# Splitting the last gather of a recurrent step into two column halves in two PSUM banks, with new issue orders, in a memory-augmented attention kernel (forward and backward)

## The chip, the cores and the metric

The kernel runs on 1 core of one Trainium2 chip. The metric is the device time of one execution in microseconds (us); lower is better. The engines named below are TensorE (PE for its matmuls, PEld for its weight loads), VectorE (DVE), ScalarE (ACT), GpSimd (POOL) and SyncE (SP); SP and POOL also issue DMA transfers, each from its own in-order queue.

## The reference, cut to what matters

The program computes a layer and the gradients of its inputs and weights: `x + A(norm(x)) + B(norm(x))`, where B is a dense layer with squared ReLU and A is attention over 64 segments of 32 tokens that hand eight memory rows from segment to segment.

```python
for s in range(n_seg):                       # 2048 / 32 = 64 segments
    h = jnp.concatenate([mem, xs], axis=1)   # 8 memory rows + 32 tokens, 512 columns
    q, k, v = h @ Wq, h @ Wk, h @ Wv         # 32 heads of 128
    p = _softmax(where(mask, q @ k.T * scale, -1e9))
    o = einsum('bhte,hed->btd', p @ v, Wo)
    mem = o[:, :M, :].copy()                 # M = 8: the next segment needs this
    outs.append(o[:, M:, :])
```

The memory rows make A a chain: a segment cannot begin its projections before the one ahead of it has finished its output projection. The gradient runs the same chain from the last segment to the first: the gradient of the eight memory rows of segment s is an input of segment s-1.

## The kernel before, in words

The program has five stages. The first normalises x and does layer B; a short one projects rows that no chain needs first. Then comes the forward chain (64 steps, one per segment), a middle stage with the rest of the attention gradient's preparation and B's weight gradients, the backward chain (64 steps), and at the end the weight gradients of A as 128 long products.

A step keeps 32 rows of one segment for four groups of eight heads, stacked to 128 partitions. Most matmuls are therefore packed: four matmuls with 32 output partitions each stand side by side in the array (`tile_position=(0, 32 * g)`), 512 columns wide. Sixteen of them make up one call of `proj` or `gather` for one half of the heads; the text calls that a unit.

A forward step is written as named operations: `k0mm k1mm q0mm q1mm v0mm v1mm` (projections, L392), `..ev` (their copies out of PSUM), `..fl` and `..Te` (turning by TensorE, L165, and copying), `s0 s1` (scores), `mx sb ex su rc pm tu` (softmax and turning of one half), `w0 w1` (products with v, L547), `oa ob` (their copies), `g0 g1` (the output projection, `gather`, L460: both halves accumulate into one PSUM tile `ps_R` of 128 x 512), `ra rb` (the copies of its two column halves to `R4`, L374 and L377, one on DVE, one on ACT), `ta tb` (two float32 turns each, L469, into the tile `ps_sum`), `HT` (the sum over the four groups of heads for the eight memory rows, written straight into the input `X` of the next step, L482) and `xt` (the same for the other rows). A backward step ends the same way: six units of `gather` (`vg kg qg`, two each) accumulate into one tile `ps_gR`, then `ra rb ta tb HT`, and the sum goes to `GT`, the input of the step that follows. Ahead of that stand `o0mm o1mm` (projection of the incoming gradient), `vp kp qp` (products), `d1 d2 d3 d4` (the softmax gradient) and the copies `ve vl ke kl qe`.

Rows that only need a block of four steps are handled by operations with the prefix `L.`: they belong to no step's chain. Their matmuls are fill for TensorE: in a forward block six projections `L.P0` to `L.P5`, two gathers `L.G0 L.G1`, `L.S W ta tb BT`; in a backward block twelve half units `L.G0` to `L.I3` and one pair of turns.

Nothing decides the order of issue at run time. `F_ORDER` and `B_ORDER` are four strings each, one per step of a block, and `play` calls the operations in the order of the strings; every engine executes its own share in that order. A `+` behind a name takes the operation of one step (or block) later, a `-` of one earlier. `ENGS` says whether a copy goes to ACT or DVE. POOL copies `pb` (the probabilities into the block-diagonal tile `PD`, which `vp` needs) and `vc`, and issues the loads `ldp ldq ldn`; SP issues the others, `vtr` and `ldk` among them. Single-buffered tiles make some of these wait: `ldq` for the last `kp` of the step ahead, `vc` for its scores, `pb` for its `vp`.

PSUM has eight banks. Four are the pool `r` (every `big` and `tr` tile: projections, scores, `ps_R`, `ps_sum`), four are the two pairs `pp0` and `pp1` for `w`, `vp`, `kp` and `qp`.

Of the kernel before, what the change touches and what calls it, by code (L numbers as in the profile page):

```python
# [26 lines left out]
def kernel(  # L27
# [372 lines left out]
    def heads_of(W):  # L400

        return lambda h: W[:, h, :]
# [50 lines left out]
    def gather(R, XT, W, h, first, last):  # L453

        for k in range(4 * h, 4 * h + 4):
            for g in range(HG):
                x, o = W(g * KH + k), R[32 * g:32 * g + 32, :]
                if len(x.shape) == 3:
                    o = o.rearrange("p (a b) -> p a b", b=P)
                nc.tensor.matmul(o, lhsT=XT(k, g), rhs=x,  # L460
                                 start=(first and k == 4 * h), stop=(last and k == 4 * h + 3),
                                 tile_position=(0, 32 * g))

# [117 lines left out]
    def play(order, n, steps, lefts, step, blk, done=None):  # L581
# [22 lines left out]
        "tb ta L.E0 HT",  # L604
        "L.W1 L.ob0 L.out- k0mm L.oa0 L.oa1 L.ob1 q0mm soP- L.E1 q1mm k0ev k1mm q0ev k0fl xt- q1ev k1ev k0Te q0fl "
        "q0Te q1fl k1fl k1Te L.hs s0 mx0 sb0 q1Te s1 v0mm mx1 sb1 ex0 v0ev su0 rc0 pm0 L.lq+ L.lp ex1 tu0 v1mm "
        "soN- su1 L.otr rc1 pm1 tu1 w0 v1ev ob0 L.P2 oa0 L.X0 w1 L.lo ob1 g0 oa1 g1 soP rb L.P3 km L.t3 ra tb ta "
        "soN HT",
        "k1mm q0mm k0mm L.E3 L.E2 kl L.sx- xt- q0ev k1ev q1mm k0ev k0fl q0fl q1ev k0Te L.hl++ k1fl q0Te L.u3 k1Te "
        "q1fl s0 mx0 q1Te s1 sb0 mx1 sb1 ex0 L.ldL+ ex1 su0 rc0 pm0 tu0 v0mm su1 v0ev rc1 pm1 v1mm L.X1 w0 v1ev "  # L610
        "tu1 oa0 ld L.G1 w1 soV- ob0 L.t2 km ob1 oa1 L.mtr g0 g1 ra L.P5 soP rb L.E5 tb ta HT",
        "L.G0 k0mm xt- L.ra q0mm kl q1mm k1mm k0ev q0ev k0fl q1ev k1ev q0fl k0Te q1fl q0Te k1fl L.u2 s0 q1Te "
        "L.lv+ L.lb k1Te L.t1 L.ta s1 mx0 sb0 mx1 sb1 v0mm ex0 ex1 v0ev v1mm su0 rc0 pm0 v1ev L.mst L.tb tu0 su1 "
        "w0 rc1 ob0 L.P4 pm1 tu1 L.xt oa0 L.E4 w1 oa1 soV- soN- g0 ob1 g1 km rb soV ra kl+ L.S0+ tb ta L.X2 soP "
        "L.u1 HT xt L.mx0+ L.S1+ L.sb0+ k0mm+ L.mx1+ q0mm+ L.sb1+ k1mm+ q1mm+ q0ev+ k0ev+ k1ev+ ld q1ev+ soN "
        "L.ex0+ k0fl+ q0fl+ k1fl+ k0Te+ q1fl+ q0Te+ L.ex1+ q1Te+ k1Te+ s0+ mx0+ v0mm+ sb0+ L.t0 L.su1+ ex0+ L.lm+ "
        "su0+ km+ s1+ mx1+ sb1+ v0ev+ ex1+ v1mm+ L.P0+ rc0+ v1ev+ pm0+ tu0+ ld++ w0+ oa0+ su1+ rc1+ pm1+ ob0+ "
        "L.P1+ tu1+ w1+ ld+ ob1+ L.su0+ L.rc0+ L.pm0+ oa1+ L.u0 L.rc1+ g0+ L.pm1+ g1+ soV+ L.tu0+ rb+ L.tu1+ "
        "L.W0+ L.BT ra+ kl++")
    ENGS = on_engines(  # L620
        "L.E1 L.E2 L.E4 L.oa0 L.ob0 k0ev k1ev oa0 ob0 ob1 q1Te q1ev rb v0ev v1ev",
        "L.E0 L.E3 L.E5 L.oa1 L.ob1 L.pm0 L.pm1 L.ra k0Te k1Te oa1 pm0 pm1 q0Te q0ev ra")
    with sb("fw", 1) as fw, psum("fr", 4) as fr, psum("fpp", 1) as fpp, \
# [182 lines left out]
        def fwd(s):  # L806
# [50 lines left out]
            for p in range(2):  # L857
# [21 lines left out]
                def G_(p=p):  # L879
                    if "R" not in ps:  # L880
                        ps["R"] = big("ps_R")
                        ps["n"] = 0
                    ps["n"] += 1
                    gather(ps["R"], lambda k, g: B_["OT"][:, g, k, j, :], heads_of(Wo), p, ps["n"] == 1, ps["n"] == 2)
                o["g%d" % p] = G_

            def ra(h):
                if "R4" not in st:
                    st["R4"] = fo.tile([P, D], F32, name="R4", tag="R4s")
                c = slice(h * 2 * P, (h + 1) * 2 * P)  # L890
                ENGS["r%s" % "ab"[h]](st["R4"][:, c], ps["R"][:, c])
            o["ra"], o["rb"] = lambda: ra(0), lambda: ra(1)
            turn_ops(o, big, lambda: st["R4"], st)

            def HTf():
                if s + 1 < NSEG:
                    b1, j1 = divmod(s + 1, SPB)
                    over_groups(block(b1)["X"][:, :, j1 * SEG:j1 * SEG + M], st["T"], slice(0, M))
            o["HT"] = HTf
            o["xt"] = lambda: over_groups(B_["XT"][:, :, j, M:SEG], st["T"], slice(M, SEG))  # L900
# [36 lines left out]
    with sb("la", 2) as la, sb("ls", 2) as ls, sb("lo", 1) as lo_, sb("wg", 2) as wg, psum("lpp", 1) as lpp, psum("lr", 4) as lr:  # L937
# [151 lines left out]
        "L.ko1 kg0 d41 qea0 L.G2 qeb0 tu1 qg0 kla0 qp1 klb0 L.I1 qea1 qeb1 kp1 qg1 keb1 kea1 klb1 kg1 rb ra L.H1 "  # L1089
        "tb kla1 vtr ta ldq HT",  # L1090
        "L.H2 o0mm L.ra1 vc- pb- o0ev o1mm L.ktr o0fl o0te o1ev vp0 ldk- xt- s0 L.kst d10 d20 vea vp1 d30 vla "
        "o1fl d40 vtr vlb vg0 veb kp0 vc tu0 vtr+ o1te ldp qp0 qeb0 s1 qea0 d11 d21 kea0 keb0 d31 vg1 qg0 kla0 "
        "klb0 d41 kg0 kp1 tu1 kea1 qp1 L.I3 keb1 qeb1 kg1 qea1 qg1 rb ra L.I2 L.vtr tb ta HT",
        "L.G3 o0mm ldn- ldk- L.ra2 o0ev kla1- o1mm o1ev ldp o0fl pb- xt- klb1- vp0 o0te s0 vea L.gs d10 vp1 vla "
# [11 lines left out]
    with sb("bq", 1) as bq, sb("bt", 1) as bt, sb("bs", 2) as bs, sb("be", 1) as be, psum("bpp", 1) as bpp, psum("br", 4) as br:  # L1106
# [111 lines left out]
        def bwd(s):  # L1218
# [40 lines left out]
            for p in range(2):  # L1259
# [51 lines left out]
                for t, n in ((2, "v"), (1, "k"), (0, "q")):  # L1311
# [13 lines left out]
                    def G_(n=n, p=p, t=t):  # L1325
                        if "R" not in ps:
                            ps["R"] = big("ps_gR")
                            ps["n"] = 0
# [215 lines left out]
```

## Time and profile before

| | |
|---|---|
| runs | 3069.1 us median of 3 (3064.48 to 3072.56) |
| span of the profiled execution | 3059.8 us (no other time is recorded for that execution) |
| PE busy | 2705.4 us, 88% of the span |
| DVE, ACT, POOL busy | 1319.5, 994.7, 658.0 us |
| mean granted TensorE clock | 0.971 |
| forward chain, from the first sum into `X` to the last | 318 to 1161 us, 62 steps of 13.59 us on average |
| backward chain, from the first sum into `GT` to the last | 1475 to 2394 us, 62 steps of 14.81 us on average |

The span runs from the first to the last instruction. Busy time of an engine is the union of its instructions' times; the ends of matmuls are modelled, so PE counts as busy while a result still travels. A row of the timeline gives start and length in us, the engine, the line, what is written from what, and in brackets how long the engine had been idle and who ended that.

### The profile page before, as it was taken

The page shows a single profiled execution, that of the slowest core. Times are in us where ns is not written, and L with a number is a line of the kernel's source. Part 1 is how long each engine was busy: PE and PEld are TensorE (multiplying, and loading weights), DVE is VectorE, ACT ScalarE, POOL GpSimd, SP SyncE. Part 2 cuts the span into 40 slices and gives each one's busy share as a digit, 9 for nine tenths or more (in the row PEclk, how much of TensorE's full clock was granted, in tenths as well). Part 3 has the DMA queues.
Part 4 walks back from the last instruction along what each step waited for, and adds up shares of the span by engine and source line. Part 5 has one row for each costly group of instructions (what it writes and reads, how often), then busy time and mean ns, then how long its engine had stood idle before and what let it go on. Part 6 is the DMA issues. An engine that isn't in the chain of part 4 may idle for free. (4 is left out here: it accounts for less than half of the span.)

```text
span 3059.8 us, 109712 instructions
## 1 busy us (share of the span) xinstructions
PE 2705.4 (88%) x48600; PEld 1386.8 (45%) x48600; DVE 1319.5 (43%) x3581; ACT 994.7 (33%) x2306; POOL 658.0 (22%) x1264
## 2 busy tenths in 40 slices
PE   8997899999999886877799899998989559999998
PEld 4453444444444444446444444444444224444443
DVE  5452566666666664334345444544545201100010
ACT  2422444444444444323333333333333101111111
POOL 0000000000000000113343433434343213322222
PEclk9998999999999998999999999999999879999999
DMA  9548375766767767777577676776777899898991
GB/s 257 185 146 250 101 188 161 189 181 172 190 168 182 165 157 192 229 230 220 149 173 174 190 187 164 177 203 169 176 200 175 238 192 217 194 211 207 204 207 39
DMA packets 794559, 566.78 MB, mean 185 GB/s; under 512 B 579409, under 2 KB 681570, under 8 KB 790754
## 3 DMA queue, kind: packets, MB, share of 16 engines
q1 hardware_dynamic: 748322, 430.47, 58.8%
q0 software_dynamic: 40528, 126.53, 13.5%
q8 instruction: 381, 6.24, 0.9%
q10 hardware_dynamic: 5232, 2.75, 0.4%
q14 instruction: 96, 0.79, 0.1%
HBM read 193.61 MB, written 238.56 MB: 141 GB/s over the span
## 5 line engine op out<-in xcount | busy, mean ns | idle before, releaser
L1505 PE MATMUL ps_gw<-gn,HNc 128*128 128x512 bf16 x1920 | 416.4, 379 | 0.0
L1505 PEld LDWEIGHTS <-HNc 128*128 128x128 bf16 x1920 | 187.8, 98 | 223.9
L374 ACT CAST f_N<-ps_proj 128x512 bf16<-128x512 f32 x320 | 185.9, 581 | 243.9 <-PE ps_proj L392 223.4
L1476 ACT CAST wt<-ps_gw 128x512 bf16<-128x512 f32 x128 | 74.4, 586 | 503.5 <-PE ps_gw L1505 474.4
L392 PEld LDWEIGHTS <-X 128*32 128x32 bf16 x6144 | 153.3, 97 | 161.3 <-DVE X L482 13.9
L835 POOL COPY kM<-f_kT 128x256 bf16<-128x256 bf16 x64 | 25.6, 401 | 786.7 <-DVE f_kT L377 594.9
L1459 DVE TENSOR_TENSOR gx<-ps_rows,gb 128x512 f32<-128x512 f32 x16 | 11.1, 692 | 420.5 <-PE ps_rows L1457 418.2
L1505 PE MATMUL ps_gw<-GOc,gn 128*128 128x512 bf16 x640 | 142.2, 385 | 54.8 <-DMA GOc<-S_GM 54.8
L460 PE MATMUL ps_gR<-Wk,gk 128*32 128x512 bf16 x2048 | 146.7, 386 | 19.4 <-ACT gk L374 12.9
L392 PE MATMUL ps_proj<-Wk,X 128*32 128x512 bf16 x2048 | 135.4, 384 | 12.6 <-DVE X L482 6.9
L460 PE MATMUL ps_gR<-Wq,gq 128*32 128x512 bf16 x2048 | 141.6, 382 | 1.2 <-issue 1.2
L374 ACT CAST gk<-b_pp 128x256 bf16<-128x256 f32 x192 | 68.8, 377 | 208.3 <-PE b_pp L547 146.6
L1477 POOL DMA_DIRECT2D out_dram<-wt x128 | 69.2, 541 | 309.5 <-ACT wt L1476 309.4
L1239 POOL COPY PD<-b_P 32x320 bf16<-32x320 bf16 x256 | 114.9, 449 | 95.3 <-PE b_pp L1292 64.4
L460 PE MATMUL ps_gR<-Wv,gv 128*32 128x512 bf16 x2048 | 133.4, 379 | 0.3 <-issue 0.3
L392 PE MATMUL ps_proj<-Wo,GT 128*32 128x512 bf16 x2048 | 123.9, 384 | 7.9 <-POOL GT L1203 6.7
L392 PE MATMUL ps_proj<-Wq,X 128*32 128x512 bf16 x2048 | 128.7, 382 | 0.0
L460 PE MATMUL ps_R<-Wo,OT 128*32 128x512 bf16 x2048 | 126.4, 388 | 0.0
L469 PE MATMUL ps_sum<-identF,R 128*128 128x128 f32 x512 | 102.4, 295 | 24.6 <-ACT R L374 18.4
L392 PE MATMUL ps_proj<-Wv,X 128*32 128x512 bf16 x2048 | 124.1, 378 | 0.0
L1505 PEld LDWEIGHTS <-gn 128*128 128x128 bf16 x640 | 63.4, 99 | 132.3 <-issue 59.6
L374 ACT CAST gON<-ps_proj 128x512 bf16<-128x512 f32 x128 | 74.9, 585 | 143.2 <-PE ps_proj L392 141.5
(260 smaller groups left out, 5128.0 us busy)
## 6 DMA issues: line engine op xcount, KB each, us to landing
S_A<-f_N SPq DMA_DIRECT2D x64, 512.0 KB
out_dram<-wt POOLq DMA_DIRECT2D x142, 128.0 KB, 4.6
S_A<-f_N SPq DMA_DIRECT2D x64, 256.0 KB
S_GB<-gv SPq DMA_DIRECT2D x32, 512.0 KB
S_GB<-gq SPq DMA_DIRECT2D x32, 512.0 KB
S_GB<-gk SPq DMA_DIRECT2D x32, 512.0 KB
b_kN<-S_A POOLq DMA_DIRECT2D x63, 256.0 KB, 5.0
b_qN<-S_A POOLq DMA_DIRECT2D x63, 256.0 KB, 5.4
```

The costliest lines, as they stand in the source:

```text
L374: nc.scalar.copy(out, in_)
L392: nc.tensor.matmul(o, lhsT=hT[:, dc, :], rhs=x, start=(dc == 0), stop=(dc == DC - 1), tile_position=(0, 32 * g))
L460: nc.tensor.matmul(o, lhsT=XT(k, g), rhs=x, start=(first and k == 4 * h), stop=(last and k == 4 * h + 3), tile_position=(0, 32 * g))
L469: nc.tensor.transpose(st["T"][:, c * P:(c + 1) * P], R4()[:, c * P:(c + 1) * P], identF[:])
L835: o["km"] = lambda: nc.gpsimd.tensor_copy(B_["kM"][:, :, :, lc], T["kT"][:, :, :, 0:M])
L1239: nc.gpsimd.tensor_copy(PD[32 * g:32 * g + 32, g], C["P"][32 * g:32 * g + 32, :, 0:L])
L1459: nc.vector.tensor_tensor(out=gx[:], in0=ps[:], in1=gb[:], op=ALU.add)
L1476: nc.scalar.copy(wt[:], ps[:])
L1477: pdma(dst, wt[:])
L1505: nc.tensor.matmul(ps[:], lhsT=l(rc), rhs=r(rc), start=(n == 0), stop=(n == RC_ALL - 1))
```

## The change

The tile of the last sum is split by columns, in both chains.

* `gather` takes a range of column blocks. In the forward step every gather is done as two calls (`in_halves`): 16 matmuls of 256 columns into `ps_R`, then 16 into a second tile `ps_R2` in another bank of `r`. In the backward step only the sixth gather is split: its left half ends the sum in `ps_gR`, its right half stands alone in `ps_R2`.
* The copy `ra` moves to ACT. Forward: `ra` copies `ps_R`, `rb` copies `ps_R2`, 256 columns each, both on ACT. Backward: `ra` copies all 512 columns of `ps_gR` on ACT, and `rb` becomes an addition on DVE of `ps_R2` to the right half of what `ra` wrote.
* The turns go to one tile of the pair `pp0` (forward, `f_T`) or `pp1` (backward, `b_T`), one bank for each half, and no longer to a tile of `r`.
* `HT` becomes `Ha` and `Hb`, `xt` becomes `xa` and `xb`: each sums one half of the columns.
* All eight strings of the two orders are written anew. The matmuls of the `L.` operations, the loads and the POOL copies stand in other places.

The core of the diff; of the orders one string of each chain is shown, the others are changed in the same manner.

```diff
-    def gather(R, XT, W, h, first, last):
+    def gather(R, XT, W, h, first, last, cs=slice(0, 4)):
 
         for k in range(4 * h, 4 * h + 4):
             for g in range(HG):
-                x, o = W(g * KH + k), R[32 * g:32 * g + 32, :]
-                if len(x.shape) == 3:
-                    o = o.rearrange("p (a b) -> p a b", b=P)
-                nc.tensor.matmul(o, lhsT=XT(k, g), rhs=x,
+                x = W(g * KH + k)
+                if len(x.shape) == 2:
+                    x = x.rearrange("p (a b) -> p a b", b=P)
+                nc.tensor.matmul(R[32 * g:32 * g + 32, 0:(cs.stop - cs.start) * P].rearrange("p (a b) -> p a b", b=P),
+                                 lhsT=XT(k, g), rhs=x[:, cs, :],
                                  start=(first and k == 4 * h), stop=(last and k == 4 * h + 3),
                                  tile_position=(0, 32 * g))
+
+    C01, C23 = slice(0, 2), slice(2, 4)
+
+    def in_halves(ps, alloc, XT, W, h, first, last):
+
+        for n, cs in (("R", C01), ("R2", C23)):
+            if n not in ps:
+                ps[n] = alloc("ps_" + n)
+            gather(ps[n], XT, W, h, first, last, cs)
+
+    def sum_ops(o, ps, st, R4, pair, added):
+
+        def dst():
+            if "R4" not in st:
+                st["R4"] = R4()
+            return st["R4"]
+
+        def ra():
+            n = D if added else 2 * P
+            ENGS["ra"](dst()[:, 0:n], ps["R"][:, 0:n])
+
+        def rb():
+            if added:
+                nc.vector.tensor_tensor(out=st["R4"][:, 2 * P:4 * P], in0=ps["R2"][:, 0:2 * P],
+                                        in1=st["R4"][:, 2 * P:4 * P], op=ALU.add)
+            else:
+                ENGS["rb"](dst()[:, 2 * P:4 * P], ps["R2"][:, 0:2 * P])
+
+        def tT(h):
+            if "T" not in st:
+                st["T"] = pair()
+            for c in (0, 1):
+                nc.tensor.transpose(st["T"][:, h, c * P:(c + 1) * P], st["R4"][:, (2 * h + c) * P:(2 * h + c + 1) * P],
+                                    identF[:])
+        o["ra"], o["rb"] = ra, rb
+        for h in range(2):
+            o["t%s" % "ab"[h]] = lambda h=h: tT(h)
+
+    def half_over_groups(out, T, h, rows):
+
+        with nc.allow_low_precision(reason="summed in float32, rounded once on the way out"):
+            nc.vector.tensor_reduce(out, T[:, h, 0:2 * P].rearrange("p (c g r) -> p c r g", c=2, g=HG)[:, :, rows],
+                                    axis=AX.X, op=ALU.add)
...
-        "k1mm q0mm k0mm L.E3 L.E2 kl L.sx- xt- q0ev k1ev q1mm k0ev k0fl q0fl q1ev k0Te L.hl++ k1fl q0Te L.u3 k1Te "
-        "q1fl s0 mx0 q1Te s1 sb0 mx1 sb1 ex0 L.ldL+ ex1 su0 rc0 pm0 tu0 v0mm su1 v0ev rc1 pm1 v1mm L.X1 w0 v1ev "
-        "tu1 oa0 ld L.G1 w1 soV- ob0 L.t2 km ob1 oa1 L.mtr g0 g1 ra L.P5 soP rb L.E5 tb ta HT",
...
+        "k0mm+++ L.lm+ L.E1+ xb++ q1mm+++ L.pm0+ xa++ L.out k0ev+++ q0mm+++ soP++ kl+++ L.tu0+ L.W0+ q0ev+++ "
+        "q1ev+++ k1mm+++ L.W1+ q0fl+++ L.ob0+ L.oa0+ k0fl+++ q1fl+++ k1ev+++ L.oa1+ k1fl+++ q0Te+++ q1Te+++ "
+        "k0Te+++ s0+++ k1Te+++ soN++ mx0+++ s1+++ sb0+++ mx1+++ ex0+++ L.ob1+ su0+++ v1mm+++ v0mm+++ sb1+++ "
+        "rc0+++ L.P2+ ex1+++ pm0+++ v0ev+++ km+++ tu0+++ su1+++ L.u0 rc1+++ w0+++ L.P3+ pm1+++ v1ev+++ ob0+++ "
+        "tu1+++ oa0+++ w1+++ L.X0+ g0+++ ob1+++ oa1+++ ld+++ g1+++ ra+++ ta+++ rb+++ kl++++ L.lp+ tb+++ Ha+++ "
+        "Hb+++",
...
     ENGS = on_engines(
-        "L.E1 L.E2 L.E4 L.oa0 L.ob0 k0ev k1ev oa0 ob0 ob1 q1Te q1ev rb v0ev v1ev",
-        "L.E0 L.E3 L.E5 L.oa1 L.ob1 L.pm0 L.pm1 L.ra k0Te k1Te oa1 pm0 pm1 q0Te q0ev ra")
+        "L.E1 L.E2 L.E4 L.oa0 L.ob0 k0ev k1ev oa0 ob0 ob1 q1Te q1ev ra rb v0ev v1ev",
+        "L.E0 L.E3 L.E5 L.oa1 L.ob1 L.pm0 L.pm1 L.ra k0Te k1Te oa1 pm0 pm1 q0Te q0ev")
...
-                    if "R" not in ps:
-                        ps["R"] = big("ps_R")
-                        ps["n"] = 0
-                    ps["n"] += 1
-                    gather(ps["R"], lambda k, g: B_["OT"][:, g, k, j, :], heads_of(Wo), p, ps["n"] == 1, ps["n"] == 2)
+                    x = lambda k, g: B_["OT"][:, g, k, j, :]
+                    ps["n"] = ps.get("n", 0) + 1
+                    in_halves(ps, big, x, heads_of(Wo), p, ps["n"] == 1, ps["n"] == 2)
                 o["g%d" % p] = G_
-
-            def ra(h):
-                if "R4" not in st:
-                    st["R4"] = fo.tile([P, D], F32, name="R4", tag="R4s")
-                c = slice(h * 2 * P, (h + 1) * 2 * P)
-                ENGS["r%s" % "ab"[h]](st["R4"][:, c], ps["R"][:, c])
-            o["ra"], o["rb"] = lambda: ra(0), lambda: ra(1)
-            turn_ops(o, big, lambda: st["R4"], st)
-
-            def HTf():
+            sum_ops(o, ps, st, lambda: fo.tile([P, D], F32, name="R4", tag="R4s"),
+                    lambda: fpp.tile([P, 2, 512], F32, name="f_T", tag="pp0"), False)
+
+            def HTf(h):
                 if s + 1 < NSEG:
                     b1, j1 = divmod(s + 1, SPB)
-                    over_groups(block(b1)["X"][:, :, j1 * SEG:j1 * SEG + M], st["T"], slice(0, M))
-            o["HT"] = HTf
-            o["xt"] = lambda: over_groups(B_["XT"][:, :, j, M:SEG], st["T"], slice(M, SEG))
+                    half_over_groups(block(b1)["X"][:, 2 * h:2 * h + 2, j1 * SEG:j1 * SEG + M], st["T"], h, slice(0, M))
+            for h in range(2):
+                o["H%s" % "ab"[h]] = lambda h=h: HTf(h)
+                o["x%s" % "ab"[h]] = lambda h=h: half_over_groups(B_["XT"][:, 2 * h:2 * h + 2, j, M:SEG], st["T"], h,
+                                                                  slice(M, SEG))
...
-        "L.G3 o0mm ldn- ldk- L.ra2 o0ev kla1- o1mm o1ev ldp o0fl pb- xt- klb1- vp0 o0te s0 vea L.gs d10 vp1 vla "
-        "d20 ldq- o1fl d30 d40 vlb vg0 kp0 veb tu0 o1te keb0 qp0 s1 qea0 klb0 vg1 kea0 kla0 pb d11 d21 kg0 L.sl- "
-        "d31 vc d41 tu1 qeb0 kp1 qp1 keb1 qg0 qea1 L.gl+ kea1 kg1 qeb1 qg1 rb ra tb ta L.H3 kla1 HT",
...
+        "o0mm++++ xb+++ vc+++ kla1+++ xa+++ o1mm++++ o0ev++++ o0fl++++ o1ev++++ L.ra2+ pb+++ ldn+++ vp0++++ L.I3+ "
+        "vea++++ L.gs+ o0te++++ ldp++++ s0++++ d10++++ vp1++++ d20++++ ldq+++ o1fl++++ d30++++ vg0++++ vla++++ "
+        "d40++++ vlb++++ kp0++++ o1te++++ veb++++ keb0++++ s1++++ ldk+++ L.G3+ tu0++++ qp0++++ d11++++ kea0++++ "
+        "pb++++ d21++++ L.ktr+ d31++++ vg1++++ klb0++++ L.kst+ kg0++++ d41++++ kla0++++ kp1++++ qeb0++++ tu1++++ "
+        "qp1++++ qea0++++ qea1++++ keb1++++ kea1++++ kla1++++ qg0++++ kg1++++ qeb1++++ qg1++++ ra++++ klb1++++ "
+        "rb++++ L.H3+ ta++++ Ha++++ tb++++ Hb++++",
...
     ENGS = on_engines(
-        "L.ra0 kea0 keb0 keb1 kla0 kla1 o0ev o1ev qea0 qea1 qeb0 rb vea veb vla vlb",
-        "kea1 klb0 klb1 o0te o1te qeb1 ra")
+        "L.ra0 kea0 keb0 keb1 kla0 kla1 o0ev o1ev qea0 qea1 qeb0 ra vea veb vla vlb",
+        "kea1 klb0 klb1 o0te o1te qeb1")
...
+                        x, W = lambda k, g: G4[n][:, g, k, j, :], turned_heads(Wqkv[t])
                         if "R" not in ps:
                             ps["R"] = big("ps_gR")
                             ps["n"] = 0
                         ps["n"] += 1
-                        gather(ps["R"], lambda k, g: G4[n][:, g, k, j, :], turned_heads(Wqkv[t]), p, ps["n"] == 1,
-                               ps["n"] == 6)
+                        if ps["n"] == 6:
+                            gather(ps["R"], x, W, p, False, True, C01)
+                            ps["R2"] = big("ps_R2")
+                            gather(ps["R2"], x, W, p, True, True, C23)
+                        else:
+                            gather(ps["R"], x, W, p, ps["n"] == 1, False)
                     o["%sg%d" % (n, p)] = G_
-            def ra(h):
-                if "R4" not in st:
-                    st["R4"] = bt.tile([P, D], F32, name="R4", tag="R4s")
-                c = slice(h * 2 * P, (h + 1) * 2 * P)
-                ENGS["r%s" % "ab"[h]](st["R4"][:, c], ps["R"][:, c])
-            o["ra"], o["rb"] = lambda: ra(0), lambda: ra(1)
-            turn_ops(o, big, lambda: st["R4"], st)
-
-            def HTf():
+            sum_ops(o, ps, st, lambda: bt.tile([P, D], F32, name="R4", tag="R4s"),
+                    lambda: bpp.tile([P, 2, 512], F32, name="b_T", tag="pp1"), True)
+
+            def HTf(h):
+                cs = slice(2 * h, 2 * h + 2)
                 if s > 0:
                     b1, j1 = divmod(s - 1, SPB)
-                    over_groups(gts[b1][:, :, j1 * SEG:j1 * SEG + M], st["T"], slice(0, M))
+                    out = gts[b1][:, cs, j1 * SEG:j1 * SEG + M]
                 else:
-                    ps["S0"] = bq.tile([P, DC, M], F32, name="gm0")
-                    over_groups(ps["S0"][:], st["T"], slice(0, M))
-            o["HT"] = HTf
-
-            def xtf():
-                if j == SPB - 1:
+                    if "S0" not in ps:
+                        ps["S0"] = bq.tile([P, DC, M], F32, name="gm0")
+                    out = ps["S0"][:, cs]
+                half_over_groups(out, st["T"], h, slice(0, M))
+
+            def xtf(h):
+                if j == SPB - 1 and h == 0:
                     nc.gpsimd.memset(B_["XT"][:, :, :, 0:M], 0.0)
-                over_groups(B_["XT"][:, :, j, M:SEG], st["T"], slice(M, SEG))
-            o["xt"] = xtf
+                half_over_groups(B_["XT"][:, 2 * h:2 * h + 2, j, M:SEG], st["T"], h, slice(M, SEG))
+            for h in range(2):
+                o["H%s" % "ab"[h]] = lambda h=h: HTf(h)
+                o["x%s" % "ab"[h]] = lambda h=h: xtf(h)
```

## The prediction

> **What bounds the kernel now.** I read the page first, then the windows of the two chains, then the timeline of one step's end in each, then the waits of the backward chain.
>
> ```profile
> PE 2705.4 (88%) x48600; PEld 1386.8 (45%) x48600; DVE 1319.5 (43%) x3581; ACT 994.7 (33%) x2306; POOL 658.0 (22%) x1264
> ```
> ```profile
> 318.00:1175.00 857.00, 795.16 (x18313) 408.78 (x18314) 554.45 (x1592) 376.47 (x849) 50.07 (x125) 1.00 0.67 171
> 1461.00:2394.00 933.00, 840.34 (x21376) 429.32 (x21372) 453.69 (x1296) 336.83 (x959) 355.84 (x688) 0.99 0.70 177
> ```
> After window and length come PE, PEld, DVE, ACT, POOL busy, then clock and DMA share. The change touches only these windows. PE is idle for 62 us of the forward and 93 us of the backward one; busy time includes results still travelling, so a little more than 155 us is the most to be had.
>
> End of a forward step:
> ```profile
> 884.51 1.91 PE L460 MATMUL ps_R<-Wo,OT 128*32 128x512 bf16 x32
> 886.35 1.04 PE L350 MATMUL ps_L<-Wv,XL 128*128 128x512 bf16 x4
> 886.47 0.42 DVE L377 COPY R<-ps_R 128x256 f32<-128x256 f32 x1 [1.38 <-PE ps_R L460]
> 886.98 0.37 ACT L374 COPY R<-ps_R 128x256 f32<-128x256 f32 x1 [1.90 <-DVE R L377]
> 887.41 0.66 PE L469 MATMUL ps_sum<-identF,R 128*128 128x128 f32 x4
> 887.99 1.05 PE L460 MATMUL ps_RL<-Wo,OTL 128*32 128x512 bf16 x16
> 888.10 0.29 DVE L482 TENSOR_REDUCE X<-ps_sum 128x32 bf16<-128x128 f32 x1
> 888.87 0.39 PE L392 MATMUL ps_proj<-Wk,X 128*32 128x512 bf16 x4
> ```
> The two copies of one bank come after each other. But PE is covered: a block unit (`ps_L`) stands under the copies, another (`ps_RL`) under the sum. The tail is long and mostly filled.
>
> End of a backward step, and its waits:
> ```profile
> 1918.73 1.05 PE L460 MATMUL ps_gR<-Wk,gk 128*32 128x512 bf16 x16 [0.34 <-DVE gk L377]
> 1919.60 1.04 PE L460 MATMUL ps_gR<-Wq,gq 128*32 128x512 bf16 x16
> 1920.74 0.37 ACT L374 COPY R<-ps_gR 128x256 f32<-128x256 f32 x1 [2.53 <-PE ps_gR L460]
> 1921.15 0.42 DVE L377 COPY R<-ps_gR 128x256 f32<-128x256 f32 x1 [2.14 <-ACT R L374]
> 1921.17 0.90 PE L469 MATMUL ps_sum<-identF,R 128*128 128x128 f32 x4 [0.53 <-ACT R L374]
> 1922.10 0.29 DVE L482 TENSOR_REDUCE GT<-ps_sum 128x32 bf16<-128x128 f32 x1 [0.53 <-PE ps_sum L469]
> 1922.45 0.61 PE L392 MATMUL ps_proj<-Wo,GT 128*32 128x512 bf16 x8
> ```
> ```profile
> ACT gk L374 <- PE b_pp L547: 146.1, 108, 3.6
> DVE R L377 <- ACT R L374: 137.5, 62, 4.6
> ```
> Here nothing covers the copies, and `kg` waited for a copy of `gk`. Backward has the idle time that can go.
>
> **The change, part by part.** Unit costs from rows: a unit 0.87 us (1918.73 to 1919.60), its result readable 0.25 later; 256-column copy 0.37 on ACT, 0.42 on DVE; cast of 512 columns 0.58; one turn 0.13, and DVE may start 0.43 after the last pair begins (887.41 plus 0.26 to 888.10).
>
> *Half matmuls.* Forward 32 matmuls of 512 columns become 64 of 256, that is 8 more rounds of four per step; backward 4 more. The trace has no packed 256-column gather. Nearest: the unpacked products L1045, 448 of 256 columns, took 52.6 us, and L1039, 224 of 512 columns, 52.0: 1.2% more. Of a 1.74 us gather that is 0.02 us forward, 0.01 backward: 2 us in all, which I take. The upper bound is a half that costs a whole (0.217 a round): 1.74 and 0.87 us a step, 167 us. Below zero is excluded, since the columns are the same. The weight loads are the doubt, since a round has four and half the time to hide them:
> ```profile
> 907.01 0.17 PEld L437 LDWEIGHTS <-f_qT 128*32 128x32 bf16 x16 [0.28 <-DVE f_qT L377]
> ```
> Sixteen loads of this shape span 0.17 us, four 0.03 to 0.04 of a half round's 0.108. One load alone is listed with 0.097; exposed once in each of the 12 times 64 added rounds it costs 75 us. The Trainium skill ("TensorE: Matmul & The Clock Gate", section "LDWEIGHTS (loading the stationary operand)") gives a load's ns as its columns over 1.2, which is 27 for 32 columns; four in series are an estimate of 107 ns, all of a half round, and 82 us if none of it hides. The row above disagrees: four took a third of that.
>
> *Forward tail.* Before, with the gather ending at E (884.51 plus 1.74 is 886.25), the next projection could start at E+2.2 and started at E+2.6. After: the first bank ends at E-0.43, so `ra` runs to E+0.2, `rb` from E+0.25 to E+0.62, `ta` under it, `tb` from E+0.68. The sum of 64 elements costs by the rows of 128 (0.29) and 384 (0.55) about 0.23. Both halves of the turns are one tile: in the built program `Ha` waits for the last turn of `tb` in three steps of four, and in the fourth `tb` waits for `Ha`. So `Ha` ends at E+1.34, the projection starts at E+1.4 (it takes `Ha` alone; `Hb` comes in time for its third block). The path is 0.8 shorter, but the new strings leave no unit in this tail (only `L.BT` in one step): PE idles 0.85 in it, against 0.26 before. The two units (1.74) go to the softmax and `w` waits, which idle about 1.2 a step before (0.25 before each score, 0.55 before `w0`, 0.2 before `w1`).
>
> Whole steps by the strings, each operation at the later of its engine and its inputs. The second string: projections with `L.W` to 4.1, flips to 5.3, scores 5.6 and 6.0, softmax on DVE to 8.7, `w0` 8.75, `w1` 10.0, gather 10.3 to 12.1, next step 13.5. The other three the same way: 13.6, 13.6, and 14.3 where `v` goes first. Sum 55.0, against 13.22+13.44+13.68+13.91=54.25: 0.7 a block, **+11 us** over 16 blocks, by this hand count's error -15 to +35.
>
> *Backward tail.* `ra` (512 columns, 0.58) runs from E-0.18 to E+0.4; `rb` is an addition of 256 columns, which no row shows: between a copy (0.42) and the 512-column addition L1173 (0.69); I take 0.42, half of L1173 plus overhead. It ends at E+0.9, `tb` E+0.95, sum E+1.6, next projection E+1.65. Before: 1920.47 to 1922.45, 1.98. Gain 0.3.
>
> *Backward middle.* Before, `kp1 qp1` stand right ahead of `kg1`, so the copies of `gk` between them are bare (PE's loads idle 0.83 before 1918.73). The new strings put `qp1` and `qg` between `kg0` and `kp1`, or both `kg0` and a half unit; `d1` starts 0.7 earlier because `s1` no longer stands behind `qp0`. First string: `o` to 1.74, `s0` 3.1, `d40` to 5.0, `s1` 5.4, `vg1` 6.4, `kg0` 7.25, `qp1` 8.2, `qg0`, `kp1` 9.5, `qg1`, `kg1` 10.7 to 11.5, next 13.2. The others: 13.9, 13.4, 13.7. Sum 54.2; I add 0.6, since `d4` took 0.53 instead of 0.40 under POOL copies: 54.8, against the undisturbed 13.74+14.04+14.67+14.80=57.25, or -0.6 a step. The median first term is 14.49, because `vp0` waited up to 1.4 for `PD`: POOL now makes `PD` right after the `vp` ahead, which gives another 0.1 to 0.2. Together -0.75 over 63 steps, **-47 us**, range -85 to -10.
>
> *New waits.* The turned tile moves to the `w`/`vp` banks. So `ta` waits for the copies of the banks' last users (`ob1`; `klb1 qeb1`), all done by E, and on PE the next `w`, `L.W0` or `vp1` stands behind `xa xb`, two DVE sums of 0.36 that end 0.8 to 3.0 into the step; first use is at 2.7 (`L.W0`) or 3.4 (`vp1`), whose followers on PE would share any lateness. Nothing, with 0.4 to spare at the tightest.
>
> *At nothing.* The loads move: POOL's `ldq ldn ldp` (0.54 each, 5 us to land) stand behind `pb` and `vc` (1.8 and 1.5) and are issued about 9.7 to 12 of a step, needed at 5 to 6 of the next: 2.5 us of cover, without which each late one stalls PE by its lateness. SP's `vtr` waits for `vc`, with the `ldk` loads queued behind it; POOL's own `vc` waits for scores. Five backward steps pause 2 to 2.7 us inside `qp` without a named wait; that stays.
>
> Sum: 2+11-47 is -34. The span 3059.8 becomes 3026; the median lies 9.3 above the span, so **3035 us**.
>
> **The rivals.**
> *Halves cost more (0.08, slower).* Place: the rounds of the split gathers. Against it the loads' row. For it: TensorE would be the bound then, at 88% busy. Break-even is 34 us over 768 rounds, 0.045 a round; at 0.097 the time is 3035+75-2, 3108. The Trainium skill's section on weight loads, named above, is the rule behind it.
> *Forward fill is lost (0.17, slower).* The units moved out of the tail find no idle time, because the scores' and softmax' chain is no longer than PE's work there. For it: the forward waits are only 62 us in all. Then each step pays the bare tail, 0.6, and `v` first in one of four, together +45 instead of +11; with the backward gain at its small end (-25) 3090. It decides when the forward step passes 14.1.
> *Backward bound by loads (0.15, little change).* Steps stay near 14.5 because loads land 5 us after issue whatever PE does. For it: DMA share 0.70, late `PD`. Time: 13 for the forward part and the halves, -10 to -15 from the two tails, 3068.
> *All of the backward idle goes (0.12, faster).* Forward even, backward -85: 2985.
> That the sum by halves does nothing is in the forecast already, `Ha` waiting for all turns.
>
> **How the numbers follow.** Forecast 0.48, rivals 0.08, 0.17, 0.15, 0.12. The forecast's own range is 2995 to 3058. To leave out no more than 2 in 10 the range takes in the load case and most of the fill case: 2985 to 3095. 0.3%, 9 us, is about what a measurement of this kernel tells from no change. Faster: 0.48+0.12 and half of the load case, 0.67; same 0.07; slower 0.26.
>
> **What would show it.** Right: steps between sums into `X` of 13.5 to 14.3, into `GT` of 13.2 to 13.9; split rounds of 0.11 us; no wait of one `R` copy for the other in forward; `PD` no longer awaited. Wrong: rounds over 0.15, forward steps over 14.1, or PE waiting for `b_qN`, `b_kN` or `b_vl`.

## The result, and the profile after

The changed kernel takes 3087.7 us (median of 6, 3082.0 to 3089.0) against 3066.8 for the kernel before (median of 6, 3055.3 to 3072.6): a ratio of 1.0077, 95% interval 1.0055 to 1.0098. It is slower by some 21 us, where 3035 and a gain were forecast.

The profiled execution spans 3087.2 us against 3059.8. The page's engine line:

```profile
PE 2713.8 (88%) x51534; PEld 1476.0 (48%) x51672; DVE 1305.9 (42%) x3772; ACT 1036.7 (34%) x2370; POOL 661.9 (21%) x1264
```

The windows of the two chains (window, length, PE, PEld, DVE, ACT, POOL busy, clock, DMA share):

```profile
315.00:1178.00 863.00, 790.15 (x19998) 456.16 (x20042) 514.02 (x1629) 395.63 (x899) 49.94 (x124) 0.99 0.60 165
1495.00:2424.00 929.00, 831.92 (x22081) 454.71 (x22081) 466.83 (x1403) 347.46 (x945) 353.26 (x677) 0.97 0.71 175
```

The forward chain is 20.7 us longer (first to last sum into `X`, 863.1 against 842.4), the backward chain 10.7 (second to last sum into `GT`, 915.3 against 904.6); the stages around them make up the rest, -4.0. In the backward window PE still idles for 97 us, and the granted clock fell from 0.99 to 0.97.

The end of an undisturbed forward step, without the weight loads:

```profile
395.17 1.93 PE L460 MATMUL ps_R<-Wo,OT 128*32 128x256 bf16 x64
396.77 0.75 ACT L374 COPY R<-ps_R 128x256 f32<-128x256 f32 x2 [1.02 <-PE ps_R L460]
397.20 0.82 PE L496 MATMUL f_T<-identF,R 128*128 128x128 f32 x4
398.06 0.36 DVE L505 TENSOR_REDUCE X<-f_T 128x16 bf16<-128x64 f32 x2 [2.30 <-PE f_T L496]
398.34 0.83 PE L392 MATMUL ps_proj<-Wv,X 128*32 128x512 bf16 x12 [0.32 <-DVE X L505]
```

And of an undisturbed backward step:

```profile
1883.84 0.62 PE L460 MATMUL ps_gR<-Wq,gq 128*32 128x256 bf16 x16
1884.28 0.62 PE L460 MATMUL ps_R<-Wq,gq 128*32 128x256 bf16 x16
1884.56 0.59 ACT L374 COPY R<-ps_gR 128x512 f32<-128x512 f32 x1 [1.53 <-PE ps_gR L460]
1885.18 0.42 DVE L487 TENSOR_TENSOR R<-ps_R,R 128x256 f32<-128x256 f32 x1 [1.94 <-ACT R L374]
1885.26 0.44 PE L496 MATMUL b_T<-identF,R 128*128 128x128 f32 x2
1885.74 0.23 DVE L505 TENSOR_REDUCE GT<-b_T 128x16 bf16<-128x64 f32 x1
```

Both tails are what the prediction drew: the first copy starts under the second half of the gather, 64 half matmuls take 1.93 us where 32 whole ones took 1.91, the next forward projection starts 1.24 us after the gather's end. What is new stands in PE's waits of the backward chain (us in all, times, longest):

```profile
PE b_pp L591 <- issue: 26.5, 27, 3.3
PE ps_gR L460 <- issue: 19.3, 13, 2.6
...
PE b_pp L591 <- DMA b_kN<-S_A: 6.6, 6, 2.0
PE ps_R L460 <- issue: 5.0, 4, 1.9
```

`issue` is idle time with no release that the profile can name. Five such pauses of over 1.2 us stood in the backward chain before; now there are twenty. The kernel before, for the same chain:

```profile
PE b_pp L547 <- issue: 11.6, 5, 2.7
PE b_pp L1290 <- POOL PD L1239: 10.0, 11, 1.4
```

What the pauses are can be read from the trace in three steps.

*They have a place in the instruction stream.* Number the records of PE, its weight loads and its waits in order of start: all twenty pauses begin at number 106 modulo 256; the five of before, all at 193. So PE's instructions come in blocks of 256. The page's queue list shows them arriving:

```profile
q8 instruction: 405, 6.64, 0.9%
```

405 packets of 16,384 bytes, and PE has 51534 + 51672 records and 444 of waits: 103650, or 404.9 blocks (the trace has 138 matmuls fewer than weight loads; with them it is 405.4). The page of the kernel before has 381:

```profile
q8 instruction: 381, 6.24, 0.9%
```

*The block is late.* Each pause ends 1.2 to 1.6 us after a packet of this queue has landed. One of them, on PE's timeline, and the DMA queues from 1770 to 1777 us (packets, MB, share of the 16 engines):

```profile
1776.55 0.20 PE L591 MATMUL b_pp<-gST,b_kLs 8*128 8x32 bf16 x4 [2.78 <-issue]
```
```profile
q1 hardware_dynamic: 1549, 1.94, 79.4%
q0 software_dynamic: 205, 0.39, 17.6%
q8 instruction: 1, 0.02, 0.8%
```

Gradient stores and the loads of the next step fill the engines; the block's one packet starts 3.6 us after PE has entered the block ahead, where 1.3 is the median. In 47 of 174 blocks it starts more than 2.5 us after that, and in the 2 us before those starts packets worth 37 engine-us were under way, against 21 for the others. PE meanwhile uses up a block of outer products and gathers in 3.4 to 4 us.

*The clock drops behind it.* Right behind the pause of 3.3 us at 1835.6, 32 packed matmuls of 512 columns take 3.24 us, where 32 take 1.90 at full clock:

```profile
1840.09 3.24 PE L460 MATMUL ps_gR<-Wk,gk 128*32 128x512 bf16 x32
```

Stretches at half clock in the backward chain: 13.7 us before, 47.7 after.

### The profile page after: what moved, and what is told of

It reads as the page before. It is cut to its first block, busy times and chain, and to the rows that moved or that the text cites. A ratio compares the mean times of both kernels' runs of the same rounds, so it can differ in the third digit from the quotient of the medians.

```text
span 3087.2 us, 116146 instructions
## 1 busy us (share of the span) xinstructions
PE 2713.8 (88%) x51534; PEld 1476.0 (48%) x51672; DVE 1305.9 (42%) x3772; ACT 1036.7 (34%) x2370; POOL 661.9 (21%) x1264
## 4 chain that ended last, share of the span: by engine, by line
PE 70%; DMA 10%; DVE 8%; issue 7%; ACT 3%; SPq 2%; POOL 1%; POOLq 0%; ACTq 0%; DVEq 0%
PE ps_gw L1564 17%; PE ps_proj L392 14%; PE ps_gR L460 8%; PE ps_R L460 4%; PE b_pp L591 3%; PE ps_RL L1221 2%; PE ps_L L350 2%; PE ps_tr L165 2%; DMA b_kN<-S_A 2%; PE ps_w L1090 2%; PE f_pp L591 2%; PE ps_w L1084 2%; PE f_T L496 1%; PE b_T L496 1%; PE ps_sc L437 1%
## 5 line engine op out<-in xcount | busy, mean ns | idle before, releaser
L460 PE MATMUL ps_gR<-Wk,gk 128*32 128x512 bf16 (+1 forms) x2048 | 137.6, 390 | 13.2 <-issue 12.3
L460 PE MATMUL ps_R<-Wo,OT 128*32 128x256 bf16 x4096 | 130.9, 280 | 10.3 <-DVE OT L377 5.2
L460 PE MATMUL ps_gR<-Wq,gq 128*32 128x512 bf16 (+1 forms) x2048 | 118.9, 346 | 2.8 <-issue 2.8
L460 PEld LDWEIGHTS <-OT 128*32 128x32 bf16 x4096 | 105.6, 99 | 19.5 <-DVE OT L377 6.9
```

Of the source, the lines that this page charges most:

```text
L460: nc.tensor.matmul(R[32 * g:32 * g + 32, 0:(cs.stop - cs.start) * P].rearrange("p (a b) -> p a b", b=P), lhsT=XT(k, g), rhs=x[:, cs, :], s ...
```

## The experiments

For each run: time, the kernel before beside it, ratio with interval; forward chain (62 steps, from the first to the last sum) and backward chain (61 steps, from the second to the last sum), in the profiled execution; pauses in the backward chain (number over 1.2 us, sum of those over 0.5); half-clock time there. All in us.

| run | time / before | ratio | forward | backward | pauses | half clock |
|---|---|---|---|---|---|---|
| before | 3066.8 | | 842 | 905 | 5, 13.7 | 13.7 |
| after | 3087.7 / 3066.8 | 1.0077 (1.0055-1.0098) | 863 | 915 | 20, 49.7 | 47.7 |
| k1_fwd_only | 3089.8 / 3066.9 | 1.0075 (1.0046-1.0104) | 866 | 905 | 6, 14.2 | 6.8 |
| k2_bwd_only | 3067.3 / 3066.9 | 0.9982 (0.9955-1.0010) | 844 | 912 | 17, 54.9 | 44.4 |
| k3_no_split | 3101.6 / 3066.9 | 1.0111 (1.0086-1.0137) | 867 | 915 | 15, 47.1 | 54.6 |
| k4_quiet | 3019.8 / 3066.9 | 0.9848 (0.9815-0.9882) | 866 | 839 | 1, 12.4 | 3.4 |
| k6_no_loads | 3058.2, one run | | 859 | 879 | 15, 35.1 | 34.1 |
| k7_no_stores | 3052.5, one run | | 863 | 878 | 8, 31.3 | 27.3 |
| k9_before_quiet | 3030.4 / 3067.4 | 0.9879 (0.9835-0.9922) | 844 | 873 | 1, 1.5 | 0 |
| k8_e5 | 3090.4 / 3069.7 | 1.0069 (1.0048-1.0091) | 860 | 904 | 6, 13.0 | 10.2 |
| k5_spread | 3152.1 / 3069.7 | 1.0268 (1.0241-1.0294) | 844 | 991 | 9, 25.9 | 140 |
| k10_qtr | 3070.4 / 3067.4 | 1.0005 (0.9982-1.0028) | 841 | 916 | 19, 49.5 | 51.2 |
| k11_act_queue | 3187.5 / 3061.2 | 1.0407 (1.0385-1.0429) | 842 | 1030 | 3, 11.7 | 188 |
| k12_sp_queue | 3042.9 / 3061.2 | 0.9950 (0.9932-0.9969) | 845 | 886 | 20, 48.3 | 10.2 |
| k13_before_sp | 3157.9 / 3063.1 | 1.0315 (1.0294-1.0337) | 845 | 996 | 6, 13.7 | 102 |
| k14_after_sp | 3085.8 / 3063.1 | 1.0079 (1.0061-1.0097) | 863 | 902 | 19, 53.7 | 44.3 |
| k15_p_sp | 3046.1 / 3063.1 | 0.9944 (0.9925-0.9964) | 844 | 889 | 17, 44.6 | 23.9 |

### Which chain loses

`k1_fwd_only` takes the hunks of the forward chain alone, `k2_bwd_only` those of the backward chain.

> Forward order, split and turns of the changed kernel, backward chain of the kernel before. Theory (instruction feed): each chain's loss is its own. Forward X-to-X step 13.92 us as in the changed kernel against 13.59 before, so 62 x 0.33 = +20 us; backward step 14.81 as before, 5 pauses without a named wait over 1.2 us in the backward chain: 3085 to 3092 us. Rival (the two chains disturb each other, or the loss is in the stage between them): within 8 us of the kernel before, 3060 to 3075.

> Backward order, split and turns of the changed kernel, forward chain of the kernel before. Theory: backward GT-to-GT step 14.98 as in the changed kernel against 14.81, 18 to 23 pauses of over 1.2 us without a named wait, 12 to 16 half-clock stretches, so +5 to +12 us: 3072 to 3080 us. Rival (pauses come from where the whole program's instruction blocks happen to fall, and fewer forward instructions move them): under 10 pauses and a step under 14.5, 3035 to 3055 us.

The chains don't disturb each other: forward alone costs 1.0075, as much as the whole change; backward alone is even. It has the pauses of the changed kernel with 16 blocks of instructions fewer ahead of it, so they don't depend on where the whole program's blocks happen to fall; its time is 5 us under the expectation.

### Pauses: the number of instructions, the order, or the DMA traffic

`k3_no_split` keeps both orders and takes the split away, so that `rb` is a plain copy in the backward step too; `k4_quiet` keeps every PE instruction and takes traffic away.

```diff
 k3:     def in_halves(ps, alloc, XT, W, h, first, last):
-        for n, cs in (("R", C01), ("R2", C23)):
-            ...
+        gather(ps["R"], XT, W, h, first, last)
```
```diff
 k4:     def so(...):
+        if b < NB - 1:
+            return
         dma(S_GB[b, t][...], ...)
-        o["ldq"] = lambda q=pdma: q(tile_of("qN", [P, GW])[:], rows[...])
+        o["ldq"] = lambda q=pdma: once("qN", 1, q)      # and "ldn" for kN
```

> Both orders of the changed kernel, but the last gather whole: 512 columns into one bank, both copies from it, 6144 PE instructions fewer. If the pauses come from the number of PE instructions: 381 blocks of 16 KB, under 10 pauses over 1.2 us in the backward chain (20 in the changed kernel), and what the copies lose by waiting for the whole gather, about 0.9 us a step in 128 steps, is not regained: forward step 14.4, backward 15.0, 3110 to 3160 us. If they come from the order (dense stretches of PE beside full DMA queues): still 15 to 25 pauses, forward step 14.6, backward 15.6, 3140 to 3200 us. Rival (the split buys nothing because the copies have slack): 3060 to 3090 us.

> The changed kernel with less DMA traffic in the backward chain and the same PE instructions: the S_GB stores are made for the last block alone (the tail reads that block's rows for all), and b_qN and b_kN are loaded once instead of in each of 64 steps. Theory (blocks of PE instructions land late behind bulk transfers): pauses over 1.2 us without a named wait fall from 20 to at most 5, half-clock stretches from 14 to at most 4, the backward step from 14.98 to 13.8 to 14.2 us: 62 x 0.8 to 1.2 = 50 to 75 us, 3015 to 3040 us. Rival (too many PE instructions for the feed, whatever the DMA queues do): 12 or more pauses, step over 14.6, 3065 to 3085 us. Rival (only the named wait for b_kN, 6.6 us in all, matters): 3078 to 3083 us.

Without the split the pauses stay (47.1 us in 381 blocks, 49.7 in 405): the number of instructions is not the cause. Without the traffic they go, with the same matmuls (22,079 in the window, 22,081 in that of the changed kernel), and the backward step falls to 13.75 us:

```profile
1509.00:2361.00 852.00, 804.44 (x22079) 446.28 (x22080) 464.71 (x1403) 347.26 (x945) 287.27 (x553) 1.00 0.44 101
```

The clock is 1.00, the DMA share 0.44 in place of 0.71. The rival with named loads (6.6 us for `b_kN`) is out: 76.6 us went. `k3` also prices the split: the four undisturbed forward steps sum to 55.7 with it away and 54.5 with it, 0.3 a step (the whole forward chain differs by 4 us only, with three half-clock stretches against five); the backward chain is the same either way. That is a third of the 0.9 expected, and why its time is 40 us under the order theory's.

Each half of the traffic alone:

> The changed kernel with b_qN and b_kN loaded once for all 64 backward steps (512 KB a step less on the software queue), S_GB stores kept. If the late blocks come from full DMA engines whatever fills them: a gain near the share of traffic, some 60% of what the run without either gave: backward step 14.97 to 14.1 to 14.4, 5 to 10 pauses over 1.2 us. If they come from the software queue alone: 13.8, at most 3 pauses. If from the stores alone: no change, 14.9, 18 to 22 pauses.

> The changed kernel without the S_GB stores of all blocks but the last (3 MB a block, 750 KB a step less, all of it in the block's last and first step), loads kept. Full engines whatever fills them: backward step 14.97 to 14.2 to 14.5, and the gain lies in the block's first step, 17.04 to 14.3 to 15.0; 6 to 12 pauses over 1.2 us. Stores alone: 13.8, at most 3 pauses. Software queue alone: no change.

Both give half: 36 and 37 us of the 77. So it is not one queue and not one kind of transfer; what counts is that the engines are full (`k6` has five pauses more than expected). Where a block's packet waits while they are, no trace shows. The stores matter most in the slowest step of four, into which the `S_GB` stores fall (by its units string 3, the last of a block, though the expectations call it the first): its median goes from 17.04 to 14.44 us, while the loads leave it at 16.45 and shorten the others.

The same cut in the kernel before:

> The kernel before with the same cut in DMA traffic as in the changed kernel's run with less of it (S_GB stored for the last block alone, b_qN and b_kN loaded once). Theory (the new backward order is really shorter, 54.2 against 57.25 us a block undisturbed, and full DMA engines take that away): without the traffic the order before falls only to its undisturbed step, 14.81 to 14.2 to 14.4, 25 to 40 us, 3027 to 3045 us, and the new order keeps a lead of 0.5 to 0.6 us a step. Rival (the lead never was there; whatever order runs is as fast as its traffic lets it): the step falls to 13.6 to 13.9 as in the changed kernel, 3000 to 3015 us.

The lead of the new order is real. Undisturbed, the backward chain is 873.3 us in the old order and 838.7 in the new one, 34.6 us or 0.57 a step. With full traffic the old order loses 31 us to it, the new one 77.

### The forward chain

In five blocks of the changed kernel PE waits for `OT` in the middle of the gather, 5.2 us in all, because of what stands ahead of its copy on DVE (PE's wait, then DVE's timeline):

```profile
PE ps_R L460 <- DVE OT L377: 5.2, 5, 1.6
```
```profile
448.76 0.45 DVE L450 STREAM_TRANSPOSE ET<-E 128x256 bf16<-128x256 bf16 x1
451.30 0.69 DVE L377 CAST dN<-ps_L 128x512 bf16<-128x512 f32 x1 [2.09 <-DMA S_NL<-dN]
451.90 0.41 DVE L377 CAST OT<-f_pp 128x256 bf16<-128x256 f32 x1
```

The copy `L.E5` of a block unit waits until the store from the same tile has landed; SP had issued that store only at 447.24, after a wait for another store. `k8_e5` is `k1` with one name moved:

```diff
-w1+++ L.E5+ g0+++ ob1+++ oa1+++ L.sx
+w1+++ g0+++ ob1+++ oa1+++ L.E5+ L.sx
```

> The run with the forward chain of the change alone, with one name moved: the copy of the L part's rows (L.E5, on DVE) from ahead of the two attention copies to behind them. Theory: that copy waits up to 2.1 us for the store of the rows before (7 waits, 9.5 us in the changed kernel) and the attention copy that the last gather needs stands behind it on DVE, 5.2 us of PE waits and the half-clock stretches that follow: forward step 13.95 to 13.8, 3075 to 3084 us against 3090. Rival (that wait is covered, the late blocks of instructions and half-clock stretches make the forward loss): 3086 to 3093 us.

The wait for `S_NL` falls from 7.4 us in `k1` to 1.5, PE's wait for `OT` in the gather is gone, and the chain falls from 866.0 to 859.6, but the total stays: the rival's number. The chain's 6 us are not clear of the spread either: in the six profiled executions that share the changed kernel's forward order word for word it took 859.1 to 866.1. What is left of the 17 us above the kernel before is spread out: the undisturbed steps are 54.5 a block against 54.25 (4 us); seven half-clock stretches against one, two of them in the first block and one to five in the last four blocks in every run with this order and the split, several behind waits of 1.4 to 1.8 us for the softmax (`k3` has the same waits and three stretches); late blocks, 2 us.

The stage behind the chain pays too, which neither theory counted. From the last sum into `X` to the first into `GT` the eight profiled executions with the new forward order took 317 to 325 us, the nine with the old one 311 to 318, some 7 us on average: among other things the last block's rows end 41 to 43 us after the last sum, not 37 to 38.

### Can the backward gain be had

Five attempts to move traffic, with the forward chain of before. `k5` and `k10` move names:

```diff
 k5:  string 3: L.vo0++ and L.vo1++ from its end to behind s1++++ and d11++++
 k5, k10:  L.qtr+ (string 3) and L.qst (string 0) to string 1
 k11: o["ldq"], o["ldn"]: q=nc.scalar.dma_start in place of pdma
 k12: the same with nc.sync.dma_start;  k15: ldp as well
```

> Forward of the kernel before, backward of the changed kernel, with bulk transfers moved out of the step in which the DMA engines are full all the time (the first of each block: 17.04 us median against 13.95 in the run with less traffic): the two S_GB stores of gv (1 MB) go from the end of the block's last step to its middle, the turn of b_gqL and its store from there to the second step. PE's instructions and their order are the same. Theory (a block of PE instructions lands late behind bulk transfers): that step's median falls from 16.3 to 17.0 us to 14.5 to 15.5, pauses over 1.2 us in the backward chain from 17 to 20 to under 12, mean backward step 14.92 to 14.3 to 14.6: 62 x 0.3 to 0.6 = 20 to 37 us, so 3030 to 3050 us. Rival (the feed is too slow for this order wherever the transfers lie): pauses only move, step 14.8 to 15.0, 3060 to 3075.

> Forward of the kernel before, backward of the changed kernel, the DMA turn of b_gqL and its store moved from the block's last and first step into its second, where the DMA engines stand idle for about half of the step; the S_GB stores stay where they are on SP. Theory: about 2.5 us of full engines less in the worst step of four, its median from 16.3 to 15.3 to 16.0 us, if the second step does not lose it again: 3045 to 3062 us. Rival (the engines are full for some 70% of the chain, so the late blocks only move): 3060 to 3072 us.

`k5` is a mistake in reading SP's queue. SP runs ahead and stops where data is missing; a store moved forward waits for its data all the same (SP stands 114 us in all at the `S_GB` stores, L1207, behind copies on ACT), and now the loads of `b_kLs` stand behind it:

```profile
PE b_pp L591 <- DMA b_kLs<-S_NL: 74.3, 44, 5.7
```

`k10` does shorten its step (median 16.32 to 15.85 us), and the pauses turn up in others: the rival's number. With the engines 70% busy over the chain, moved traffic meets the next blocks.

> Forward of the kernel before, backward of the changed kernel, with the loads of b_qN and b_kN issued by ACT (a hardware queue) in place of POOL (the software queue): the same bytes at about the same places. The two slowest starts of an instruction block in the changed kernel's backward chain (6.9 and 5.9 us after PE entered the block before) fell where the 4096-byte packets of the software queue alone filled the engines. Theory (full engines, whatever fills them): pauses 45 to 60 us in sum as with POOL, 54.9, step 14.9: 3060 to 3075 us; ACT, 37% busy, has room for two issues a step. Rival (the software queue is what the blocks wait behind): pauses under 25 us, step 14.2 to 14.5, 3025 to 3045 us.

> The same, with the two loads issued by SP, in line with the S_GB stores and the turns, so that these are not on the engines at the same time. Theory (full engines): the total of pauses stays at 45 to 60 us, and loads now stand behind SP's waits for the data of stores, so that waits for b_kN or b_qN of 0.3 us a step or more come up: 3070 to 3100 us. Rival (two queues at once hold up the third, the instruction queue): pauses under 30 us and no more than 5 us of new waits, 3030 to 3050 us.

`k11` fails for a reason that neither theory had: ACT issues a load when its own program gets there, POOL and SP run ahead. In the median a load is issued 3.9 us before PE first uses it, against 9 to 10 us from POOL (`k2`) and 8 to 9 from SP (`k12`). The loads come late, and PE waits for them by name:

```profile
PE b_pp L591 <- DMA b_qN<-S_A: 65.4, 38, 5.7
PE b_pp L591 <- DMA b_kN<-S_A: 55.7, 27, 4.9
```

`k12` beats both kernels, by 0.3 to 0.7% against before, and does so against both expectations: no new waits for loads, and nearly the same pauses. Its time lies in the rival's range, but the rival wanted pauses under 30 us. Of the 26 us that its backward chain gains on `k2`, 6.6 are shorter pauses; the half-clock time falls by 34 us, worth about 17. Three more runs ask whose gain that is:

> The kernel before with the loads of b_qN and b_kN issued by SP instead of POOL. If the new backward order is what the other queue brings out: no gain here, since only 14 us of pauses are to be had; its own waits for PD (POOL) may shrink: 3045 to 3070 us. If issuing from SP is good by itself: a gain of about 20 us as in the new order, 3035 to 3045, and then the new order is worth nothing with either queue. If the order before puts the loads behind SP's waits for stores: new waits for b_kN or b_qN, 3075 to 3110 us.

> The changed kernel, whole, with the loads of b_qN and b_kN issued by SP. If the gain of the same edit with the forward of before (3043 against 3067 us, 912 to 886 us for the backward chain, the sum of pauses 55 to 48 and the half-clock time 44 to 10 us) belongs to the backward chain: 915 to 885 to 895 us, and 3060 to 3070 us in all. If it came from where the half-clock stretches happened to fall: 3080 to 3090 us, 10 or more half-clock stretches in the backward chain.

> Forward of the kernel before, backward of the changed kernel, with b_qN, b_kN and b_P (128 KB) all issued by SP. If bulk on one queue leaves more room to the instruction blocks: pauses from 48 to 30 to 42 us, 3030 to 3040 us. If P then stands behind the waits for stores, PD comes late and vp waits for it: 3050 to 3080 us.

In the order before the same edit costs 91 us of chain: there a load stands ahead of the stores and waits for PE, the stores come late, and the copies that overwrite the stored tile wait in DVE's and ACT's queues, by DVE's waits:

```profile
DVE gq L377 <- DMA S_GB<-gq: 94.7, 15, 6.8
```

So issuing from SP is not good by itself. `k15` repeats the gain with the new backward order (889 us of chain) without adding to it, between its two expectations. In the whole changed kernel (`k14`) it is not confirmed. The backward chain of the profiled execution gains 13 us, half of what was expected, with no fewer pauses and about as much half-clock time; but the stages around the chains are as much longer there, and the time, 1.0079 of the kernel before against 1.0077 without the edit, is that of the other expectation, with its ten or more half-clock stretches (44.4 us, thirteen). How much of the gain of `k12` and `k15` is the queue's and how much lies in where the half-clock stretches fell stays open.

## Why the prediction was wrong

*Half matmuls, 2 us.* Right: 1.93 us for 64 halves, no exposed weight loads. The rival of exposed loads is out, and with it the time that went with the rule of the Trainium skill named beside it.

*Forward tail and steps, +11.* The undisturbed steps were walked well (55.0 forecast, 54.5 measured, 54.25 before), and `Ha` waits for all turns as read from the program. The chain still lost 20.7, inside the term's own -15 to +35 but not by its sum: the term had no place for a wait on DVE behind a store (5 us on PE), for late instruction blocks (4) and for the half-clock stretches, nor for the 7 us of the stage behind the chain. No run takes these apart cleanly, so the shares stay readings of the trace. The rival "forward fill is lost", 3090, has the time almost to the us, but not its mechanism: it was to decide at steps over 14.1, and they are 13.9 on average, 13.6 in the median.

*Backward tail and middle, -47.* The walked steps hold: 54.2 a block forecast, 53.8 the sum of the shortest step of each kind, 53.9 the sum of the medians in `k4`. `rb` took the 0.42 that was taken for it, PE no longer waits for `PD`. The runs with little traffic give the order 34.6 us, inside the range of -85 to -10 and 12 short of the -47.

*The failed step* is the last sentence of "At nothing": "Five backward steps pause 2 to 2.7 us inside `qp` without a named wait; that stays." It did not stay. The pauses were a queue at its limit: blocks of 256 PE instructions behind bulk transfers, with the idle time of the old order as their cover. The new order took that cover away: blocks used up in under 4 us rose from 28 of 166 to 45 of 174, and blocks whose packet starts more than 2.5 us after PE has entered the block ahead from 32 to 47. Pauses went from 13.7 to 49.7 us and half-clock time from 13.7 to 47.7, and the sums close roughly on the runs with little traffic, whose own pauses are taken off: 37 of pauses, 22 for the clock (half of 44) and 7 for `b_kN` are 66 of the 77 us that the new order loses; 12, 7 and 10 for `PD` are 29 of the 31 of the old. The row that would have warned was on the page: DMA share 0.70 in the window that was to be made denser.

*The rivals.* "Backward bound by loads" named the full DMA engines but not the path: it expected late data, and the waits for `b_kN` are 6.6 us. PE waiting for `b_kN` was one of the signs named as wrong.

*The loads, new waits in the `w` and `vp` banks.* At nothing, as said, but for that 6.6.

## What to carry to other kernels

A pause of the busiest engine without a named wait is a cost that grows when its neighbourhood gets denser: look whether such pauses lie a fixed number of instructions apart, and whether the DMA engines are full there, before booking the gain of a tighter order. A hand-walked step gives the floor; what is left of it must be sought in what shares the DMA engines, and one run with some traffic left out prices that in one look. In queues that run ahead, a moved DMA doesn't move in time, it moves relative to what waits behind it.

## What the runs showed of the hardware

PE's instructions come by DMA in blocks of 16 KB and share the 16 engines with data. The Trainium skill ("Runtime: NRT & Kernel Launch", section "Instruction fetch mechanics") has refills in blocks of 256 instructions, and the trace agrees: 404.9 blocks, 405 packets. It calls the cost of crossing a boundary mostly hidden; in this kernel it is 50 us of pauses, with blocks used up in 3.4 us while the engines are full.

Half clock often follows short holes. In the two chains of all seventeen traces, a half-clock stretch began within 8 us of the start of a PE hole of 1.4 to 1.6 us in 10 of 38 cases, of one of 1.6 to 1.9 in 32 of 63, of one of 1.9 to 3.6 in 100 of 131; for holes of 0.5 to 1.4 us it was 117 of 1269. It is no certainty: in `k12` it was 2 of 10 of the holes over 1.9 us. A single stretch lasts 3.41 us and costs a step about 1.6 (two forward steps of one string in the changed kernel, 14.98 us each against 13.41 for the median of the others). The Trainium skill ("TensorE: Matmul & The Clock Gate", section "HAM oscillation — how this bites in real kernels") gives "no PE-idle gaps >~3.4µs" as the rule; here holes of about 2 us, in a PE that is 88% busy, were followed by half clock in most cases, and the measurement decides.
